# Six slots from chunk 3 to chunk 2, three from chunk 4 to chunk 3, chunk 3 turned by matmuls, and a new order of all queues

## Chip, core and metric

The kernel runs on one core of a Trainium2 chip. The metric is the device time of one execution in microseconds (us). An execution takes a little longer than the span of its trace, which runs from the first to the last instruction.

## The reference, cut to what matters

The inputs are x, r_gate and i_gate (4 x 5056 x 256), a_param (256), and a layer of 8 experts with 1024 hidden features, all float32.

```python
a    = exp(8 * sigmoid(r_gate) * log(sigmoid(a_param)))      # per token and feature
g    = sqrt(max(1 - a*a, 1e-6)) * sigmoid(i_gate) * x
h[t] = a[t] * h[t-1] + g[t]                                  # along the 5056 tokens of a sequence
e_idx = argmax(h @ w_gate)                                   # one of 8 experts for each token
out   = softmax(h @ w_gate)[e_idx] * sigmoid(h @ w_output_gate)[e_idx]
        * (relu(h @ w1[e_idx]) @ w2[e_idx])                  # 20224 tokens, 256 -> 1024 -> 256
```

## The kernel before, in words

**Chunks.** The 20224 tokens are 158 tiles of 128, worked in chunks: chunks 0 and 1 have 4 tiles each, every further one 8. For a chunk, SP loads r, i and x (L752). ACT makes the gates (L758, L761), the decay (L768), its square (L772) and the root (L777; ACT needs another function table for it). DVE multiplies (L764, L780) and runs the scan (L812). PE and DVE then find a power-of-two scale (for the first four chunks L836, L842, L845, L852 to L859).

**Turning rows.** The scan has features on the partitions, while the slots gather tokens as rows of `rows_all`, in two float16 parts (high and low). There are two ways. Chunks below `BY_PE` are turned by matmuls with a stationary scan tile and a moving identity (`project`, L932), which brings the routing logits with it. ACT takes the high part out of PSUM (L948) and DVE the low part (L951, L952). The other chunks are split in place by ACT (L972) and DVE (L977, L979), SP turns the halves by a transposing DMA, called a flip below (L988), and PE makes the logits by other matmuls (L996), gathered by DVE (L1004). Either way 12 tile rows of `rows_all` take turns.

**Routing.** DVE and ACT choose the expert and its probability (L1035 to L1080), PE counts ranks (`pk`, L1053, L1055), DVE makes positions (L1086 to L1093), and POOL scatters the 8 tiles' rows to `xs` in HBM, by expert (L545).

**Slots.** A slot is up to 128 rows (256 in the later sets) of one expert. SP fetches it with a transposing DMA (L1234) and its scales (L1235). A table `SETS` has entries (chunk, first expert, end expert, rows): one slot of so many rows for each of the experts, which may start once the chunk of that number is scattered. Chunks are counted from 0, here and below, so `(3, 0, 8, 128)` is a slot for each expert behind the fourth chunk. Rows that are left go to 16 end slots and 3 half end slots of 64 rows (`ENDS`, `HALVES`). The slots of set 0 (slots 0 to 7) are plain: they use the expert's weights in float32 as they are loaded (L1276, L1292, L1327, L1367). The others use two float16 parts: 48 matmuls L1306, relu on ACT (L1331), low part on DVE (L1334), 24 matmuls L1381 for each 128 rows, result on ACT (L1402), store by POOL (L1405).

**Weights.** Unit 2e is w1 of expert e, unit 2e+1 its w2. Each is loaded (L601, by ACT's queue for the first seven, by SP for the others), squared up on PE, ACT and DVE (`pg`: L627, L633, L636, L641) to find its scale, and split on ACT and DVE (L669, L679). Units 14 and 15 are loaded in four pieces (`fw14_0` to `fw15_1`) into the ring of the plain slots' hidden tiles.

**Order.** Every queue is worked in the order in which it was filled. The works are collected first; `places` gives each a rank from a table, and `in_order` lists them by rank with a model of the engines' time.

Of the kernel before, what the change touches and what calls it, by code (L numbers as in the profile page):

```python
# [1534 lines left out]
```

## Time and profile before

| | |
|---|---|
| median of 3 runs | 1009.37 us (1009.24 to 1009.70) |
| profiled execution | 1010.89 us |
| its span, granted TensorE clock | 1009.0 us, 0.977 of full |
| PE busy | 940.9 us (93%) |
| DVE, ACT, POOL busy | 678.2, 624.1, 359.9 us |

The chain that ended last is made of PE to 59%, DVE 13%, ACT 11% and DMA 10%. PE's last matmul ends at 1000.35 us and its first slot starts at 69.25 us. Read the page's 40 slices from left to right: PE is filled from the fourth on, with one dip in the slice from 126 to 151 us, where PEclk falls to 8 tenths too. Clock 0.50 in a stretch is the lower of two levels, 1.2 and 2.4 GHz.

### The profile page before, as it was taken

What the parts mean: (1) busy time and instruction counts of PE and PEld (TensorE: products, weight loads), DVE (VectorE), ACT (ScalarE), POOL (GpSimd) and SP (SyncE); (2) the same over time, 40 slices, a digit from 0 to 9 for tenths busy, and PEclk for the clock granted to TensorE, in tenths of its full rate; (3) what the DMA queues carried; (4) which work ended last, traced back from release to release, by engine and by line L of the source; (5) the groups of instructions that cost most, each with busy time, mean ns of one, the idle gap of its engine ahead of it and who ended that gap; (6) DMA issues with size and microseconds to landing.
All of it is one profiled execution on the core that took longest, in us unless ns stands there. A gap on an engine that the chain in (4) does not pass through costs nothing.

```text
span 1009.0 us, 27629 instructions
## 1 busy us (share of the span) xinstructions
PE 940.9 (93%) x10796; PEld 860.5 (85%) x10796; DVE 678.2 (67%) x1719; ACT 624.1 (62%) x931; POOL 359.9 (36%) x341
## 2 busy tenths in 40 slices
PE   1389959999999999999999999999999999999996
PEld 1379859998999899999888888988888888899994
DVE  5789998888978898889878987878322222322231
ACT  8799987877777688877778777743322322322321
POOL 2115252544444444445344554444221211221111
PEclk9779988999999999999999999999999999999998
DMA  9999997989999999899988898656522122138771
GB/s 318 338 264 330 241 211 184 218 191 221 212 222 200 209 253 255 166 228 221 249 179 224 203 250 210 122 125 208 113 52 53 48 54 49 47 111 229 247 232 37
DMA packets 269237, 189.75 MB, mean 188 GB/s; under 512 B 211071, under 2 KB 222080, under 8 KB 269104
## 3 DMA queue, kind: packets, MB, share of 16 engines
q1 hardware_dynamic: 249488, 138.37, 59.5%
q0 software_dynamic: 15408, 42.22, 13.7%
q10 hardware_dynamic: 4208, 7.34, 2.0%
q8 instruction: 88, 1.44, 0.6%
q14 instruction: 45, 0.37, 0.1%
HBM read 79.09 MB, written 44.82 MB: 123 GB/s over the span
## 4 chain that ended last, share of the span: by engine, by line
PE 59%; DVE 13%; ACT 11%; DMA 10%; issue 4%; POOL 1%; SPq 1%; ACTq 0%; POOLq 0%; DVEq 0%
PE po L1381 27%; PE ph L1306 27%; DMA out_dram<-ot,osc 3%; DVE it L812 3%; DVE h L1334 3%; DMA it<-in_i_gate_dram 3%; PE po L1367 2%; DVE it L780 2%; ACT it L772 2%; ACT it L777 1%; ACT L777 1%; PE ph L1292 1%; DVE peak L864 1%; DVE xt L764 1%; DMA fw<-in_moe_w_dram 1%
## 5 line engine op out<-in xcount | busy, mean ns | idle before, releaser
L1381 PE MATMUL po<-w2r,h 128*128 128x256 f16 (+2 forms) x3720 | 494.5, 273 | 2.8 <-ACT ot L1402 1.3
L1306 PE MATMUL ph<-xt,w1r 128*128 128x128 f16 (+1 forms) x4608 | 427.1, 241 | 3.9 <-DMA xt<-xs 3.0
L1381 PEld LDWEIGHTS <-h 128*128 128x128 f16 (+1 forms) x3720 | 347.5, 98 | 41.9 <-issue 3.5
L1306 PEld LDWEIGHTS <-w1r 128*128 128x128 f16 x4608 | 349.2, 98 | 30.5 <-DMA xt<-xs 3.4
L1334 DVE SCALAR_TENSOR_TENSOR h<-ph,h 128x512 f16<-128x512 f32 (+1 forms) x310 | 208.3, 680 | 225.6 <-ACT h L1331 222.8
L1331 ACT ACTIVATE h<-ph 128x512 f16<-128x512 f32 (+1 forms) x310 | 180.6, 588 | 253.0 <-PE ph L1306 156.6
L1405 POOL DMA_INDIRECT out_dram<-ot,osc x163 | 174.9, 1073 | 424.7 <-ACT ot L1402 367.0
L545 POOL DMA_INDIRECT xs<-rows_all,posi x158 | 180.0, 1139 | 207.5 <-ACT h L1331 93.9
L1402 ACT ACTIVATE ot<-po,osc 128x256 f32<-128x256 f32 (+1 forms) x163 | 73.2, 469 | 62.2 <-PE po L1381 41.1
L812 DVE TENSOR_TENSOR_SCAN it<-rt,last,it 128x512 f32<-128x512 f32 (+4 forms) x78 | 96.1, 1241 | 0.5
L780 DVE SCALAR_TENSOR_TENSOR it<-it,xt 128x1024 f32<-128x1024 f32 (+1 forms) x40 | 48.3, 1208 | 28.9 <-ACT it L777 28.9
L768 ACT ACTIVATE rt<-rt,lam 128x512 f32<-128x512 f32 (+1 forms) x80 | 62.5, 803 | 2.4 <-issue 1.7
L1306 PE MATMUL ph<-xt,ws 128*128 128x128 f16 (+1 forms) x912 | 63.8, 215 | 0.0
L764 DVE SCALAR_TENSOR_TENSOR xt<-it,xt 128x1024 f32<-128x1024 f32 (+1 forms) x40 | 48.2, 1205 | 18.1 <-ACT it L761 18.1
L1306 PEld LDWEIGHTS <-ws 128*128 128x128 f16 x912 | 55.8, 98 | 4.1 <-issue 2.0
L761 ACT ACTIVATE it<-it 128x1024 f32<-128x1024 f32 (+1 forms) x40 | 41.5, 1040 | 16.1 <-DMA it<-in_i_gate_dram 16.1
L979 DVE SCALAR_TENSOR_TENSOR rt<-it,scale,rt 128x512 f16<-128x512 f32 (+1 forms) x76 | 48.9, 685 | 1.9 <-ACT rt L972 1.8
L772 ACT ACTIVATE it<-rt 128x1024 f32<-128x1024 f32 (+1 forms) x40 | 41.6, 1044 | 10.0 <-DVE xt L764 9.2
L758 ACT ACTIVATE rt<-rt 128x1024 f32<-128x1024 f32 (+1 forms) x40 | 41.7, 1043 | 9.3 <-DMA rt<-in_r_gate_dram 9.0
L777 ACT ACTIVATE it<-it,quarter 128x1024 f32<-128x1024 f32 (+1 forms) x40 | 44.8, 1134 | 0.3
L972 ACT ACTIVATE rt<-it,scale 128x1024 f16<-128x1024 f32 (+1 forms) x38 | 42.0, 1131 | 4.2 <-DVE scale L886 4.1
L864 DVE TENSOR_REDUCE peak<-it 128x1 f32<-128x1024 f32 (+1 forms) x34 | 40.0, 1193 | 0.0
(186 smaller groups left out, 694.1 us busy)
## 6 DMA issues: line engine op xcount, KB each, us to landing
rt<-in_r_gate_dram SPq DMA_DIRECT2D x39, 512.0 KB
it<-in_i_gate_dram SPq DMA_DIRECT2D x39, 512.0 KB
xt<-in_x_dram SPq DMA_DIRECT2D x39, 512.0 KB
ws<-w1r SPq DMA_DIRECT2D x38, 512.0 KB
w1r<-in_moe_w_dram ACTq DMA_DIRECT2D x4, 1024.0 KB
w2r<-in_moe_w_dram SPq DMA_DIRECT2D x4, 1024.0 KB
w2r<-in_moe_w_dram ACTq DMA_DIRECT2D x3, 1024.0 KB
w1r<-in_moe_w_dram SPq DMA_DIRECT2D x3, 1024.0 KB
```

Source lines behind the costliest of these rows:

```text
L545: op = nc.gpsimd.indirect_dma_start(out=xs[:, :], out_offset=bass.IndirectOffsetOnAxis(ap=pos, axis=0), in_=rows.bitcast(F32), in_offset=None,
L768: nc.scalar.activation(r[:, h], r[:, h], AF.Exp, scale=lam[:, h:h + 1], bias=lam[:, h:h + 1])
L772: nc.scalar.activation(t("it"), t("rt"), AF.Square)
L777: nc.scalar.activation(t("it"), t("it"), AF.Sqrt, scale=-0.25, bias=quarter)
L780: nc.vector.scalar_tensor_tensor(t("it"), t("it"), 0.5e-3, t("xt"), op0=ALU.max, op1=ALU.mult)
L812: nc.vector.tensor_tensor_scan(H[:, h, lo:hi], A[:, h, lo:hi], H[:, h, lo:hi], first, op0=ALU.mult, op1=ALU.add)
L1306: nc.tensor.matmul(ph[:, i, 0:w], lhsT=ws[:, f // 2 % 2, a, c, f % 2 * P:(f % 2 + 1) * P], rhs=xt[:, b * ND + c, 0:w], start=n == 0, stop= ...
L1331: newest["relu"] = nc.scalar.activation(part(0, f0), tiles["ph", s, f0][:, :, 0:w], AF.Relu).ins
L1334: nc.vector.scalar_tensor_tensor(part(1, f0), tiles["ph", s, f0][:, :, 0:w], 0.0, part(0, f0), op0=ALU.max, op1=ALU.subtract)
L1381: nc.tensor.matmul(po[0:pw, j], lhsT=hh[:, a, f % 4, j * P:j * P + pw], rhs=second(b), start=f + j + a + b == 0, stop=f == NF - 1 and a == ...
L1402: nc.scalar.activation(ot[0:pw], tiles["po", s][0:pw, j], AF.Copy, scale=tiles["osc", s][0:pw, j, 0:1])
L1405: op = nc.gpsimd.indirect_dma_start(out=out[:, :], out_offset=bass.IndirectOffsetOnAxis(ap=tiles["osc", s][0:pw, j, 1:2].bitcast(I32), axi ...
```

## The change

- `SETS`: (2, 0, 6, 128) gives experts 0 to 5 their second slot after chunk 2, where all eight had it after chunk 3; experts 6 and 7 keep theirs, and experts 3 to 5 get their third slot after chunk 3 too, where all eight had it after chunk 4; experts 0 to 2 and 6, 7 keep it there. All 104 such slots stay. Slots 8 to 13 are the six, 14 and 15 the two, 16 to 18 the three.
- `BY_PE` is a tuple: chunk 3 is turned by matmuls too.
- `ENDS` 16 to 19 and `HALVES` 3 to 0: the three half end slots have 128 rows.
- `PLAIN` names the same set. Line numbers fall by 5 from L752 on.
- `laid_out` reads the order of emission itself from a table; `in_order` is left for the loop after it only.

```diff
-SETS = [(1, 0, 8, 128), (3, 0, 8, 128), (4, 0, 8, 128), (5, 0, 8, 128), (6, 0, 8, 128), (8, 0, 8, 128), (9, 0, 8, 128), (10, 0, 8, 128),
+SETS = [(1, 0, 8, 128), (2, 0, 6, 128), (3, 6, 8, 128), (3, 3, 6, 128), (4, 0, 3, 128), (4, 6, 8, 128), (5, 0, 8, 128), (6, 0, 8, 128), (8, 0, 8, 128), (9, 0, 8, 128), (10, 0, 8, 128),
         (12, 0, 8, 256), (14, 0, 8, 256), (16, 0, 8, 256), (18, 0, 8, 256), (20, 0, 8, 256)]
-PLAIN = (0,)
+PLAIN = {0: 0}
-BY_PE = 2
+BY_PE = (0, 1, 3)
-ENDS = 16
-HALVES = 3
+ENDS = 19
+HALVES = 0
...
-        for b in range(0, nt, 4) if c < BY_PE else ():
+        for b in range(0, nt, 4) if c in BY_PE else ():
...
-    first = [w for w in works if not w.late]
-    for w, v in zip(first, places(len(first))):
-        w.rank = v
-
     engines = {PE, mybir.EngineType.Activation, mybir.EngineType.DVE}
     with tc.manual_schedule(engines=engines):
-        for w in in_order([w for w in works if not w.late], {"DVE": 1.7, "ACT": 0.8}):
-            w.emit()
+        for k in laid_out(len([w for w in works if not w.late])):
+            works[k].emit()
```

**ACT's queue at chunk 1.** Before; `rt_2_4`, `it_2_4` belong to chunk 2, `lg_1_0` and `prow_1_1` to `prow_1_3` to chunk 1, whose high parts are the four L948:

```order
L768 ACTIVATE rt_2_4_159<-rt_2_4_159,lam_94 128x512
L761 ACTIVATE it_2_4_273<-it_2_4_273 128x1024 [waits DMAHW4_49]
L601 DMA w1r_135<-in_moe_w1_dram 128x2x1024 [waits DMAHW2_49]
L948 ACTIVATE rows_all_134<-lg_1_0_339,scale_1_376 128x256 [waits DVE_49,PE_49]
L948 ACTIVATE rows_all_134<-prow_1_1_363,scale_1_376 128x256 [waits PE_49]
L948 ACTIVATE rows_all_134<-prow_1_2_280,scale_1_376 128x256
L948 ACTIVATE rows_all_134<-prow_1_3_319,scale_1_376 128x256
L772 ACTIVATE it_2_4_273<-rt_2_4_159 128x1024 [waits DVE_49]
L772 ACTIVATE it_2_0_154<-rt_2_0_156 128x1024
L1039 ACTIVATE ex_1_403<-df_1_401 128x32 [waits DVE_49]
L777 ACT_TABLE_LOAD
L777 ACTIVATE it_2_0_154<-it_2_0_154,quarter_92 128x1024 [waits Activation_49]
```

After; L943 is the high part, L756 the gate i, L596 a weight load:

```order
L763 ACTIVATE rt_2_4_193<-rt_2_4_193,lam_94 128x512
L756 ACTIVATE it_2_0_164<-it_2_0_164 128x1024
L943 ACTIVATE rows_all_131<-lg_1_0_342,scale_1_376 128x256 [waits DVE_49,PE_49]
L943 ACTIVATE rows_all_131<-prow_1_1_373,scale_1_376 128x256 [waits PE_49]
L943 ACTIVATE rows_all_131<-prow_1_2_380,scale_1_376 128x256 [waits PE_49]
L943 ACTIVATE rows_all_131<-prow_1_3_386,scale_1_376 128x256 [waits PE_49]
L596 DMA w2r_133<-in_moe_w2_dram 128x8x256 [waits DMAHW3_49]
L756 ACTIVATE it_2_4_283<-it_2_4_283 128x1024 [waits DMAHW2_49]
L628 ACTIVATE dg_2_423,sq_2_424<-pg_2_398 128x128 [waits PE_49,Activation_49]
L767 ACTIVATE it_2_0_164<-rt_2_0_161 128x1024 [waits DVE_49]
L1034 ACTIVATE ex_1_434<-df_1_429 128x32 [waits DVE_49]
L763 ACTIVATE rt_2_4_193<-rt_2_4_193,lam_94 128x512
```

The four high parts stood behind the gate of `it_2_4`, which waits for its load, and behind a weight load. Now both stand behind them.

**PE's queue behind slot 7.** Before; `ph_7` is slot 7, `lg_4` are logits of chunk 4:

```order
L1292 MATMUL ph_7_4_1520<-xt16_7_1305,fw14_1_1456 128x128
L1292 MATMUL ph_7_4_1520<-xt16_7_1305,fw14_0_1438 128x128
L1292 MATMUL ph_7_4_1520<-xt16_7_1305,fw14_1_1456 128x128
L996 LDWEIGHTS rt_4_0_828
L996 MATMUL lg_4_0_1451<-g16_101,rt_4_0_828 128x48 [waits DVE_49]
L996 LDWEIGHTS rt_4_0_828
L996 MATMUL lg_4_0_1451<-g16_101,rt_4_0_828 128x48
L996 LDWEIGHTS rt_4_0_828 [waits DVE_49]
L996 MATMUL lg_4_0_1451<-g16_101,rt_4_0_828 128x32
```

After; `ph_8` is layer 1 of slot 8 (L1301), `lg_4_0<-dp_4` finds chunk 4's scale:

```order
L1287 MATMUL ph_7_4_1490<-xt16_7_1263,fw14_0_1404 128x128
L1287 MATMUL ph_7_4_1490<-xt16_7_1263,fw14_1_1415 128x128
L872 LDWEIGHTS ones_b_97
L872 MATMUL lg_4_0_1512<-dp_4_1500,ones_b_97 128x128 [waits DVE_49]
L1301 LDWEIGHTS w1r_132 [waits DMAHW4_49]
L1301 MATMUL ph_8_0_1514<-xt16_8_1425,w1r_132 128x128 [waits PE_49]
L1301 LDWEIGHTS w1r_132
L1301 MATMUL ph_8_0_1514<-xt16_8_1425,w1r_132 128x128
L1301 LDWEIGHTS w1r_132
```

Logits that wait for DVE stood behind slot 7. Now slot 8, of chunk 2's set, stands there, 36 matmuls of it in a row, and the logits come later.

**SP's queue between the fetches of slots 5 and 7.** Before; L988 are the flips of chunk 3:

```order
L1234 DMA_TRANSPOSE xt16_5_1074<-xs_84 128x4x128 [waits DMAHW0_49,DVE_49,PE_49]
L1235 ISA
L1235 DMA mt_5_1075<-xs_84 128x2 [waits DMAHW1_49]
L752 DMA it_4_4_1137<-in_i_gate_dram 128x2x512 [waits DMAHW2_49,DVE_49,Activation_49]
L988 DMA_TRANSPOSE rows_all_134<-rt_3_0_243 128x19x128 [waits DMAHW3_49,DVE_49,Activation_49]
L1223 TENSOR_LOAD firsti_0_447
L1234 ISA
L1234 DMA_TRANSPOSE xt16_6_1230<-xs_84 128x4x128 [waits DMAHW4_49,PE_49]
L1235 ISA
L1235 DMA mt_6_1231<-xs_84 128x2 [waits DMAHW5_49]
L988 DMA_TRANSPOSE rows_all_134<-rt_3_4_283 128x19x128 [waits DMASW5_49,DMASW4_49,DMAHW6_49,DMASW3_49,DMASW2_49]
L1223 TENSOR_LOAD firsti_0_447
```

After, from slot 5's fetch on:

```order
L1229 DMA_TRANSPOSE xt16_5_976<-xs_84 128x4x128 [waits DMAHW3_49,DVE_49,PE_49]
L1230 ISA
L1230 DMA mt_5_977<-xs_84 128x2 [waits DMAHW4_49]
L747 DMA xt_4_0_1026<-in_x_dram 128x2x512 [waits DMAHW5_49]
L747 DMA it_4_4_1044<-in_i_gate_dram 128x2x512 [waits DMAHW6_49,PE_49]
L596 DMA w1r_132<-in_moe_w1_dram 128x2x1024 [waits DMAHW7_49]
L747 DMA xt_4_4_1070<-in_x_dram 128x2x512 [waits DMAHW0_49]
L596 DMA w2r_133<-in_moe_w2_dram 128x8x256 [waits DMAHW1_49]
L1218 TENSOR_LOAD firsti_0_475
L1229 ISA
L1229 DMA_TRANSPOSE xt16_6_1129<-xs_84 128x4x128 [waits DMAHW2_49,DVE_49,PE_49]
```

The two flips are gone; loads of chunk 4 and of weights stand in their place.

## Rows read from the trace of the kernel before

**Rows 1.** By stretch: us; busy PE, PEld, DVE, ACT, POOL; PEclk, DMA share, GB/s.
```profile
60.00:130.00 70.00, 66.58 (x621) 62.26 (x620) 65.19 (x151) 66.84 (x97) 22.69 (x18) 0.97 1.05 266
130.00:160.00 30.00, 19.21 (x172) 17.00 (x171) 25.61 (x43) 25.18 (x30) 11.34 (x6) 0.77 0.91 202
...
300.00:700.00 400.00, 398.11 (x4710) 364.17 (x4708) 338.50 (x866) 288.55 (x421) 186.12 (x170) 1.00 0.89 205
```

**Rows 2.** Timeline of ACT (start, duration, instruction, idle before and releaser).
```profile
36.88 1.06 ACT L761 ACTIVATE it<-it 128x1024 f32<-128x1024 f32 x1 [1.68 <-DMA it<-in_i_gate_dram]
36.89 3.71 ACTq L601 DMA_DIRECT2D w1r<-in_moe_w_dram  x1
40.70 0.47 ACT L948 ACTIVATE rows_all<-lg,scale 128x256 f16<-128x256 f32 x1 [2.76 <-issue]
...
46.75 1.28 ACT L1067 ACT_TABLE_LOAD   x1
```

**Rows 3.** Timeline of PE at the first slot.
```profile
66.80 1.69 PE L627 MATMUL pg<-w1r 128*128 128x128 bf16 x16
...
69.25 3.82 PE L1292 MATMUL ph<-xt,w1r 128*128 128x128 f32 x32
```

**Rows 4.** Timeline of PE, its five waits between 130 and 160 us.
```profile
134.78 0.64 PE L627 MATMUL pg<-fw 128*128 128x128 bf16 x8 [1.80 <-DMA fw<-in_moe_w_dram]
...
143.66 0.21 PE L996 MATMUL lg<-g,rt 128*128 128x32 bf16 x1 [3.95 <-DVE rt L979]
144.32 0.61 PE L996 MATMUL lg<-g,rt 128*128 128x32 bf16 x13 [0.45 <-DVE rt L979]
146.73 1.46 PE L1306 MATMUL ph<-xt,w1r 128*128 128x128 f16 x12 [1.81 <-DMA xt<-xs]
...
151.84 1.03 PE L627 MATMUL pg<-fw 128*128 128x128 bf16 x8 [2.79 <-DMA fw<-in_moe_w_dram]
```

**Rows 5.** By stretch, in slices of 5 us.
```profile
140.00:145.00 5.00, 0.82 (x14) 0.61 (x14) 5.00 (x10) 4.66 (x6) 1.33 (x1) 0.82 0.67 157
145.00:150.00 5.00, 2.32 (x20) 2.05 (x20) 4.86 (x11) 3.88 (x5) 1.23 (x1) 0.50 0.98 166
150.00:155.00 5.00, 3.16 (x15) 2.76 (x16) 1.71 (x4) 1.93 (x4) 0.00 (x0) 0.50 0.82 115
```

**Rows 6.** Timeline of PE, turning by matmuls (L932) and logits behind flips (L996).
```profile
31.39 0.71 PE L932 MATMUL lg<-iw,it 128*128 128x144 f32 x4
31.93 0.65 PE L932 MATMUL prow<-iw,it 128*128 128x144 f32 x4
...
98.94 0.62 PE L996 MATMUL lg<-g,rt 128*128 128x48 bf16 x16
```

**Rows 7.** Timeline of SP's queue, a flip of chunk 3 and a load.
```profile
102.26 6.98 SPq L988 DMA_TRANSPOSE rows_all<-rt  x1
...
118.19 0.39 SPq L752 DMA_DIRECT2D rt<-in_r_gate_dram  x1
```

**Rows 8.** Timeline of PE, full end slots, then the last half slot.
```profile
953.45 0.49 PE L1381 MATMUL po<-w2r,h 128*128 x3
953.78 1.50 PE L1306 MATMUL ph<-xt,ws 128*128 128x128 f16 x24
955.12 0.49 PE L1381 MATMUL po<-w2r,h 128*128 x3
...
991.64 0.35 PE L1306 MATMUL ph<-xt,ws 128*128 128x64 f16 x6
...
995.90 4.45 PE L1381 MATMUL po<-w2r,h 128*64 x36
```

**Rows 9.** Timeline of POOL and SP: last scatter of chunk 8, first fetch of its slots.
```profile
319.34 0.97 POOL L545 DMA_INDIRECT xs<-rows_all,posi  x1 [0.31 <-DVE osc L1349]
...
329.53 1.57 SPq L1234 DMA_TRANSPOSE xt<-xs  x1
```

**Rows 10.** Timeline of POOL, first scatter of chunk 2.
```profile
86.95 0.97 POOL L545 DMA_INDIRECT xs<-rows_all,posi  x1 [2.92 <-DVE osc L1349]
```

More of the change, by code (lines that the diff above doesn't have):

```diff
@@ L336, in rglru_moe @@
     NF = F // P
-    assert GRAMS >= BY_PE and D == 2 * P and E == 8 and F == 8 * P and N % P == 0 and N + (FILLS + 1) * P <= REGION and max(w for *_, w in SETS) <= FILLS * P
+    assert GRAMS > max(BY_PE) and D == 2 * P and E == 8 and F == 8 * P and N % P == 0 and N + (FILLS + 1) * P <= REGION and max(w for *_, w in SETS) <= FILLS * P
     chunks = []
@@ L744, in load @@
                 bufs = rings[tags[k]].n
-                wide_ = c >= BY_PE and tags[k] == PLANES
+                wide_ = c not in BY_PE and tags[k] == PLANES
                 t = pool.tile(
@@ L854, in level @@
             )
-            if c >= BY_PE:
+            if c not in BY_PE:
                 inv = small.tile([P, 1], I32, name=f"inv_{c}", tag="inv")
@@ L901, in chunk @@
             en = work("PE", 0.25, energy, [mo], EARLY + c / 100, uses=[pu0], slack=SLACK[c > 4])
-            le = work("DVE", 0.3 + 0.15 * (c >= BY_PE), level, [en], late_rank, uses=[pu0])
+            le = work("DVE", 0.3 + 0.15 * (c not in BY_PE), level, [en], late_rank, uses=[pu0])
         else:
@@ L1213, in slot @@
         ready, vuse = planned[s] if expert is None else (counted[c], again_used[group])
-        plain = set_of[s] in PLAIN
+        plain = expert is not None and expert >= PLAIN.get(set_of[s], E)
         scaled = None if expert is None or plain else undone[expert]
@@ L1326, in relu @@
                         tiles["hh", s, 0] = wk.tile([P, NF, P], F32, name=f"h_{s}", tag="hh")
-                    newest["relu"] = nc.scalar.activation(tiles["hh", s, 0][:, f0:f0 + g], tiles["ph", s, f0], AF.Relu).ins
+                    newest["relu"] = nc.scalar.activation(tiles["hh", s, 0][:, f0:f0 + g, 0:w], tiles["ph", s, f0][:, :, 0:w], AF.Relu).ins
                     return
@@ L1346, in scales @@
             again = tiles["again", s][0:pw] if expert is None else tiles["again", group][0:pw, place, 0:q]
-            by = tiles["scale", s][0:pw] if expert is None else 1.0 if plain else tab[:, 2, expert:expert + 1]
+            by = tiles["scale", s][0:pw] if expert is None else 1.0 if plain else tab[0:pw, 2, expert:expert + 1]
             nc.vector.tensor_scalar(osc[0:pw, 0:q, 0:1], tiles["mt", s][0:pw, 0:q, 0:1], by, None, op0=ALU.mult)
@@ L1367, in multiply2 @@
                     nc.tensor.matmul(
-                        po[:, 0], lhsT=tiles["hh", s, 0][:, f], rhs=raw_of(2 * expert + 1, f * D, D), start=f == 0, stop=f == NF - 1,
+                        po[0:pw, 0], lhsT=tiles["hh", s, 0][:, f, 0:w], rhs=raw_of(2 * expert + 1, f * D, D), start=f == 0, stop=f == NF - 1,
                     )
```

143 lines of the change are left out of this document (69 added, 74 removed).

## The prediction

> **What bounds the kernel now.** I read the busy time by stretch first [rows 1]. From 300 to 700 us PE works 398.11 of 400 us at full clock: there every microsecond of PE work counts, and no wait is left to win. From 60 to 130 us it works 66.58 of 70. The exception is 130 to 160 us, with 19.21 of 30 and a clock of 0.77. So time can come from three places: before the first slot, in this hole, or from the amount of PE's work.
>
> The timeline of PE in the hole [rows 4] shows five waits, 1.80 + 3.95 + 0.45 + 1.81 + 2.79 = 10.80 us, all of the idle time there. Two are for pieces of the last expert's weights (`fw`, 4.59 us), two for the split of chunk 4 on DVE (4.40 us), one for the first rows of the slots behind chunk 3 (1.81 us). The clock is the second loss [rows 5]: behind the long wait it falls to 0.82 and then to 0.50, the lower level of 1.2 GHz. What work there was ran slower: 0.82 x 0.18 + (2.32 + 3.16) x 0.50 = 2.9 us. The hole costs 13.7 us.
>
> Before the first slot I read the timelines of ACT and PE. The slot's layer 1 starts at 69.25 [rows 3], behind the routing of chunk 1. That routing waits at 36.88 on ACT, where the gate of chunk 2 waits 1.68 us for its load, and the high parts of chunk 1 wait another 2.76 us behind a weight load that holds ACT's queue for 3.71 us [rows 2]. Later it waits again, for a table load of 1.28 us at 46.75.
>
> **The change part by part.** The sums are made against the profiled execution, 1010.89 us with a span of 1009.0. It is 1.5 us above the median of the runs, so I take 1.5 off at the end.
>
> *Start.* In the new ACT order the four high parts of chunk 1 stand ahead of that gate and that weight load. The waits ahead of them were 1.68 + 2.76 = 4.44 us [rows 2]. The probability sum `zs` also stands ahead of the table switch, which saves its reload, 1.28 us. Together 5.7 us. Against it, three weight loads in a row now stand on ACT ahead of the high parts of chunk 0, each behind the landing of an earlier transfer; the one such issue that the rows show took 3.71 us. Ends: 5.7 us won, 3.7 us lost. Slot 0 also follows, on PE, the squares of unit 6 at 66.80 [rows 3]; if their weights land no earlier, only 69.25 - 66.80 = 2.5 us can be won without them. I take 4.0 won: nearer the ACT rows, because the waits there are seen, and because slot 0 no longer needs what stood ahead of chunk 1. From 60 to 130 us PE is 95% busy [rows 1], so a shift at its beginning is carried to the hole.
>
> *The hole.* Six slots behind chunk 2 can now fill it. Chunk 2's scatter begins at 86.95 [rows 10], some 50 us ahead of the hole, so these rows are not waited for. In the PE order slot 8 stands right behind slot 7, and the logits of chunk 4 come later. The two waits for DVE (4.40) and the one for rows (1.81) go: 6.2 us. What is late next there is `fw`: slot 7 still needs its weights, and the second piece of w2 needs the buffer of `fw14_0`, free only after slot 7's layer 1. I leave both waits in, 4.59 us; if they go too, the sum is that much lower. With two short waits and float16 slots between them I expect the clock to hold: 2.9 us. The hole gives 6.2 + 2.9 = 9.1 us, between 6.2 (the clock falls anyway) and 13.7.
>
> *Chunk 3 by matmuls.* Four records of L932 make one tile, and two batches start 31.93 - 31.39 = 0.54 us apart [rows 6]: 8 tiles, 4.3 us. The logits that fall away are 32 of L996, and 16 took 0.62 us: 1.2 us. PE gets 3.1 us more, all on the path, since the stage around it is 95% filled. On ACT eight high parts of about 0.4 to 0.47 us [rows 2] stand against two wide ones, one to two microseconds more; DVE's low parts take about what the split and the gathering took. Neither is on the path while slots wait in stock.
>
> *Flips.* One held SP's queue for 6.98 us, a load for 0.39 us [rows 7]. I give their removal nothing: the waits for `fw` are waits for buffers, and the other waits of the hole are counted already. If the free queue brought the weights earlier, it would win the 4.59 us above; if loads merely go out into a full DMA, nothing. The Trainium skill (Advanced Engine Details and Errata, X-Bar Transpose (TRN2)) says that transposing DMAs are as fast as regular ones, which would make the removal worth no more than dropping a load of the same size. The rows show the queue held far longer, though not how long the bytes took. By the rule the sum stays as it is; by the rows it could be 4.6 us lower.
>
> *Ends.* The last half slot: from 991.64 to 995.90 run 48 of L1306 and 15 of L1381, and 36 of L1381 take 4.45 us, 0.124 each [rows 8]. So the 48 take 4.26 - 15 x 0.124 = 2.4, and a half slot 2.4 + 24 x 0.124 = 5.4 us. A full one: 24 of L1306 take 955.12 - 953.78 = 1.34, three of L1381 953.78 - 953.45 = 0.33, so 48 and 24 take 2.7 + 2.6 = 5.3 us. Halving the rows saved nothing; three full ones for three half ones cost 0, within 0.3 us either way.
>
> *Order of the rest.* From 300 us on PE has under 0.5% idle [rows 1]. A new order can lose there, hardly gain; I take 0.
>
> Sum: 1010.9 - 4.0 - 9.1 + 3.1 = 1000.9, less 1.5: **999.4**. Its own range is 993 (the `fw` waits go too, full start gain) to 1004 (clock falls, half the start gain).
>
> **The rivals.**
> - *Supply gives the lead back.* PE arrives some 10 us earlier at every later chunk, while DVE, ACT and DMA must keep up. The tightest place I found is chunk 8: its last scatter starts at 319.34 and takes 0.97, the first fetch of its slots is at 329.53 [rows 9]: 9.2 us of slack. If DVE and ACT don't come earlier at all, the lead ends at 9.2 us; if they come later by the 4 us of the longer queues and matmul turning, at 5.2, so 1009.4 - 5.2 = 1004.2. For it: DMA is 0.89 busy there. Against: DVE has 61 of 400 us free [rows 1], and most scatters wait for pacing, not for rows.
> - *No gain.* The start stays, because PE waits for weights of unit 6 instead, and in the hole the `fw` waits grow by what the others lose, 6.2 us. Then only the clock, 2.9, stands against 3.1: 1009.6.
> - *Slower.* The high parts of chunk 3 need the `rows_all` places of chunk 2's first tiles, so they wait on ACT for scatters that begin at 86.95 [rows 10], and behind them wait weight splits and a relu of the plain slots. It decides if PE brings chunk 3's tiles before that. Waiting from some 79 to 87 costs 8 us at a place where PE has no stock; with 3.1 for the matmuls, the start unmoved, and the hole's 6.2 won back: 1009.4 + 8 + 3.1 - 6.2 = 1014.3.
> - *More work on the fullest engine.* PE is the fullest engine, and 3.1 us are added to it; if PE's idle time only moves elsewhere, the result is 1009.4 + 3.1 = 1012.5. The Trainium skill (Perfetto Trace Analysis, Identifying the Most-Contended Engine) says to optimize the engine of highest occupancy first, and by that work should leave PE. The hole in rows 1 speaks against its use here: PE is not full in the stage that gets the work.
>
> **How the numbers follow.** Forecast 0.60 (993 to 1004), supply 0.13 (about 1004), no gain 0.10 (1008 to 1011), slower by ACT's wait 0.10 (1014), slower by added work 0.07 (1012). The first two are faster, and a third of the third: 0.76. A measurement of this kernel can tell 0.2%, 2 us, from no change; same 0.07, slower 0.17. The range that leaves out two in ten runs from 990 to 1011: it cuts both slower cases and some of the low end.
>
> **What would show it.** Slot 0 near 65 us, and the high parts of chunk 1 on ACT without the 4.4 us ahead of them. In the hole no wait for DVE's split or for rows, slot 8 right behind slot 7, clock 1.00 throughout, and at most two waits for `fw`. Eight L932 tiles of 0.54 us. After 300 us idle time of PE of 2 us, as before. I am wrong if PE waits for rows of chunk 8 or 9, if ACT waits for a scatter at chunk 3's high parts while PE idles, or if the first slot starts after 69 us.

## The result

The changed kernel took 999.55 us (median of 4, 999.23 to 1002.18), the kernel before beside it 1009.54. The ratio is 0.9903, with a 95% interval of 0.9882 to 0.9924. The profiled execution took 999.23 us with a span of 997.5 us, 11.5 us less than the 1009.0 us of before; the medians are 10.0 us apart, since the profiled execution of before was 1.5 us above its median.

The same view by stretch as in [rows 1] (columns: us; busy PE, PEld, DVE, ACT, POOL; granted clock, DMA share, GB/s), of the changed kernel:

```profile
60.00:130.00 70.00, 67.75 (x583) 62.39 (x583) 65.40 (x141) 64.67 (x95) 26.28 (x17) 1.00 0.92 256
130.00:160.00 30.00, 26.91 (x342) 24.04 (x342) 29.06 (x74) 27.17 (x37) 13.70 (x11) 1.00 0.95 211
160.00:300.00 140.00, 135.54 (x1952) 126.84 (x1950) 128.86 (x325) 111.96 (x157) 67.12 (x61) 1.00 0.99 231
300.00:700.00 400.00, 396.95 (x4638) 363.42 (x4636) 330.21 (x842) 291.25 (x422) 183.97 (x168) 1.00 0.86 198
```

From 130 to 160 us PE works 26.91 us where it worked 19.21, and the clock is 1.00 where it was 0.77. The last two rows show the price. From 160 to 300 us the row of before was this one:

```profile
160.00:300.00 140.00, 137.04 (x1971) 128.94 (x1969) 120.16 (x306) 106.20 (x152) 64.45 (x57) 1.00 0.91 204
```

There DVE is now busy 128.86 us for 120.16, and PE has 4.46 us without work where it had 2.96. From 300 to 700 us PE has 3.05 us without work where it had 1.89.

PE's time without work, stretch by stretch of the same view, adds up to the result:

| stretch, us | before | changed | difference |
|---|---|---|---|
| 0 to 130 | 43.7 | 36.4 | -7.3 |
| 130 to 160 | 10.8 | 3.1 | -7.7 |
| 160 to 700 | 4.9 | 7.5 | +2.7 |
| 700 to the end | 8.8 | 8.4 | -0.4 |
| PE busy | 940.9 | 942.1 | +1.2 |
| span | 1009.0 | 997.5 | -11.5 |

PE's timeline behind slot 7, which answers to [rows 4]:

```profile
126.95 0.63 PE L622 MATMUL pg<-fw 128*128 128x128 bf16 x8 [0.21 <-DMA fw<-in_moe_w_dram]
...
129.71 3.73 PE L1287 MATMUL ph<-xt,fw 128*128 128x128 f32 x32
133.28 0.22 PE L872 MATMUL lg<-dp,ones_b 128*128 128x128 bf16 x1
133.34 0.50 PE L1301 MATMUL ph<-xt,w1r 128*128 128x128 f16 x6
135.36 1.83 PE L1301 MATMUL ph<-xt,w1r 128*128 128x128 f16 x30 [1.52 <-ACT h L1322]
137.03 1.27 PE L622 MATMUL pg<-fw 128*128 128x128 bf16 x16
...
140.85 0.49 PE L991 MATMUL lg<-g,rt 128*128 128x32 bf16 x13 [0.31 <-DVE rt L974]
```

Slot 7's layer 1 (L1287) is followed by slot 8's (L1301). The wait for the last weights is 0.21 us where 1.80 and 2.79 stood, the wait for DVE's split 0.31 where 3.95 and 0.45 stood, and nothing waits for rows. One new wait is there: 1.52 us at 135.36 for ACT, where a relu frees PSUM.

The start:

```profile
58.68 3.60 PE L1287 MATMUL ph<-xt,w1r 128*128 128x128 f32 x24 [0.28 <-DVE xt L1271]
```

Slot 0 begins at 58.68 us, 10.6 us before 69.25 [rows 3].

### The profile page after: what moved, and what is told of

Read it like the earlier page. It is cut to its first block, busy times and chain, and to the rows that moved or that the text cites. A ratio compares the mean times of both kernels' runs of the same rounds, so it can differ in the third digit from the quotient of the medians.

```text
span 997.5 us, 27694 instructions
## 1 busy us (share of the span) xinstructions
PE 942.1 (94%) x10796; PEld 863.5 (87%) x10796; DVE 684.5 (69%) x1739; ACT 630.4 (63%) x941; POOL 360.2 (36%) x340
## 4 chain that ended last, share of the span: by engine, by line
PE 65%; DVE 4%; DMA 3%; ACT 3%; issue 2%; POOL 0%; SPq 0%; POOLq 0%; ACTq 0%; DVEq 0%
PE ph L1301 32%; PE po L1376 32%; DMA it<-in_i_gate_dram 2%; DVE it L807 1%; DMA out_dram<-ot,osc 1%; PE lg L991 1%; DVE h L1329 1%; ACT h L1326 1%; ACT rt L967 1%; DVE it L775 0%; ACT it L772 0%; ACT L772 0%; DVE peak L859 0%; DMA xs<-rows_all,posi 0%; ACT it L767 0%
## 5 line engine op out<-in xcount | busy, mean ns | idle before, releaser
L1376 PE MATMUL po<-w2r,h 128*128 128x256 f16 (+1 forms) x3720 | 491.3, 272 | 2.3 <-DVE h L1329 1.7
L1301 PE MATMUL ph<-xt,w1r 128*128 128x128 f16 (+1 forms) x4608 | 426.2, 241 | 5.2 <-DVE h L1329 2.3
L1376 PEld LDWEIGHTS <-h 128*128 128x128 f16 x3720 | 348.2, 98 | 42.6 <-DVE h L1329 3.9
L1301 PEld LDWEIGHTS <-w1r 128*128 128x128 f16 x4608 | 350.7, 98 | 32.2 <-issue 4.7
L1329 DVE SCALAR_TENSOR_TENSOR h<-ph,h 128x512 f16<-128x512 f32 x310 | 210.0, 686 | 225.6 <-ACT h L1326 225.0
L1326 ACT ACTIVATE h<-ph 128x512 f16<-128x512 f32 x310 | 181.8, 593 | 263.7 <-PE ph L1301 191.8
L1400 POOL DMA_INDIRECT out_dram<-ot,osc x163 | 183.5, 1126 | 386.5 <-ACT ot L1397 328.0
L540 POOL DMA_INDIRECT xs<-rows_all,posi x158 | 171.7, 1087 | 235.2 <-ACT h L1326 99.0
L1397 ACT ACTIVATE ot<-po,osc 128x256 f32<-128x256 f32 x163 | 73.1, 469 | 50.6 <-PE po L1376 37.4
L1301 PE MATMUL ph<-xt,ws 128*128 128x128 f16 x912 | 68.9, 219 | 0.0
L1301 PEld LDWEIGHTS <-ws 128*128 128x128 f16 x912 | 60.1, 98 | 2.6
L759 DVE SCALAR_TENSOR_TENSOR xt<-it,xt 128x1024 f32<-128x1024 f32 (+1 forms) x40 | 48.3, 1208 | 14.9 <-ACT it L756 13.9
L767 ACT ACTIVATE it<-rt 128x1024 f32<-128x1024 f32 (+1 forms) x40 | 41.8, 1045 | 11.1 <-DVE xt L759 10.8
L756 ACT ACTIVATE it<-it 128x1024 f32<-128x1024 f32 (+1 forms) x40 | 41.7, 1043 | 11.0 <-DMA it<-in_i_gate_dram 9.1
L967 ACT ACTIVATE rt<-it,scale 128x1024 f16<-128x1024 f32 (+1 forms) x36 | 39.5, 1130 | 3.4 <-DVE scale L881 3.3
```

The costliest lines, as they stand in the source:

```text
L540: op = nc.gpsimd.indirect_dma_start(out=xs[:, :], out_offset=bass.IndirectOffsetOnAxis(ap=pos, axis=0), in_=rows.bitcast(F32), in_offset=None,
L759: nc.vector.scalar_tensor_tensor(t("xt"), t("it"), 1.0, t("xt"), op0=ALU.add, op1=ALU.mult)
L967: nc.scalar.activation(halves(key, 0, m // P), of_tiles(key, m), AF.Copy, scale=tiles["scale_of", c])
L1301: nc.tensor.matmul(ph[:, i, 0:w], lhsT=ws[:, f // 2 % 2, a, c, f % 2 * P:(f % 2 + 1) * P], rhs=xt[:, b * ND + c, 0:w], start=n == 0, stop= ...
L1326: newest["relu"] = nc.scalar.activation(part(0, f0), tiles["ph", s, f0][:, :, 0:w], AF.Relu).ins
L1329: nc.vector.scalar_tensor_tensor(part(1, f0), tiles["ph", s, f0][:, :, 0:w], 0.0, part(0, f0), op0=ALU.max, op1=ALU.subtract)
```

## The experiments

Twelve runs were made in three groups of four. A group shares a chip and its runs of the kernel before, and the chips differ: that kernel took 1018.6 us in the first group, 1019.96 in the second and 1008.55 in the third. All ratios are to the kernel before of the same group. Two groups hold the changed kernel itself as a control; the first doesn't, and its ratios can only be held against a control of another chip. Where an order is changed, the diff names the works in the order of emission.

**Controls: the changed kernel again.** No edit.

> The changed kernel itself, as a control beside the three below, since chips differ: the four runs before this one stood beside runs of the kernel before that took 1018.6 us, not 1009.4. Theory A: a chip shifts both kernels alike, so the ratio is 0.990 again. Rival: the gain rests on transfers and waits that take other times on another chip; then the ratio lies nearer to 1 (0.995 to 1.003).

> The changed kernel once more, as control of this group, on a chip that may be another one. Theory S, the supply gives the lead back: the start and the hole are won on every chip (PE idle ahead of 160 us lower by 12 to 14 us than in the kernel before), and how much of it is left at the end depends on how fast chunks are made behind 160 us; so the ratio lies anywhere from 0.990 to 1.002, with PE's idle time between 160 and 700 us higher in proportion: 7.5 us at 0.990, about 20 us at 1.00. Rival: the start or the hole themselves differ between chips.

Measured: on the second group's chip 1019.27 us, ratio 1.0015 (0.9991 to 1.0039), so no gain at all; on the third's 999.11 us, ratio 0.9906 (0.9884 to 0.9928), the result again. The kernel before is slower on the second chip too, by 11.4 us (1019.96 for 1008.55). Here are the two controls by stretch, the one without the gain first:

```profile
0.00:60.00 60.00, 25.96 (x210) 23.18 (x211) 44.54 (x146) 48.73 (x68) 11.04 (x26) 0.83 0.93 322
...
130.00:160.00 30.00, 26.59 (x335) 23.79 (x334) 29.02 (x68) 26.12 (x36) 13.50 (x10) 1.00 0.88 209
160.00:300.00 140.00, 129.80 (x1821) 119.85 (x1820) 122.80 (x320) 105.70 (x147) 64.95 (x58) 1.00 0.94 218
300.00:500.00 200.00, 193.76 (x2626) 178.83 (x2624) 163.98 (x400) 153.85 (x215) 87.63 (x80) 1.00 0.96 210
500.00:700.00 200.00, 196.41 (x1971) 175.36 (x1969) 159.40 (x398) 139.44 (x208) 92.86 (x83) 1.00 0.77 183
```

```profile
0.00:60.00 60.00, 25.61 (x213) 22.95 (x214) 44.18 (x146) 48.40 (x68) 11.04 (x26) 0.89 0.92 322
...
130.00:160.00 30.00, 26.81 (x342) 24.05 (x342) 29.06 (x74) 27.19 (x37) 13.69 (x11) 1.00 0.94 211
160.00:300.00 140.00, 135.95 (x1961) 127.43 (x1959) 129.34 (x328) 112.66 (x158) 67.69 (x62) 1.00 0.98 231
300.00:500.00 200.00, 197.85 (x2623) 184.31 (x2622) 171.90 (x433) 157.76 (x221) 88.40 (x81) 1.00 0.96 215
500.00:700.00 200.00, 200.00 (x2019) 179.78 (x2017) 159.43 (x416) 133.45 (x201) 95.98 (x87) 1.00 0.77 184
```

Ahead of 160 us PE is without work for 41.0 us in the first and 40.4 in the second (3.5 and 2.8 of it from 60 to 130 us), against 54.4 in the kernel before: start and hole are won on either chip. Behind it the chips part: from 160 to 700 us 10.2 + 6.2 + 3.6 = 20.0 us in the first and 4.1 + 2.2 = 6.2 us in the second. When theory S was written, the second chip's 20 us and the 7.5 us of the result were already known, so the one new number is the 6.2 us at a ratio of 0.9906, and it fits. The kernel with full ends below, which stands for the kernel before on the second chip, has 53.2 us ahead of 160 us and 11.5 from 160 to 700: of the 12 us won there, 8.5 are given back behind 160 us, and 3 go into PE's busy time. The gain differs by some 10 us between this chip and that of the result: 5.8 of them lie from 160 to 700 us, 2.8 ahead of 160 us and 2.0 in PE's busy time.

What PE waited for from 160 to 700 us (waits by line: us in total, times, longest; the second chip's control, then the changed kernel of the result):

```profile
PE ph L1301 <- issue: 6.3, 12, 1.2
PE ph L1301 <- DVE h L1329: 5.8, 11, 1.0
PE po L1376 <- issue: 3.6, 9, 1.2
```

```profile
PE ph L1301 <- DVE h L1329: 2.3, 5, 1.0
```

On the second chip 10.2 us are waits for nothing that the profile shows ("issue"); the full-ends kernel has 6.0 us of them there, the changed kernel of the result none. 5.8 us are waits for the low parts that DVE makes, and none is for rows. So it isn't shown that transfers are slower on that chip, and why the lead is given back there is open.

**The start alone.**

```diff
 kernel before, order of emission
-its own, throughout
+that of the changed kernel up to slot 0's first matmul, then its own
```

> The kernel before with one part of the change: the order of emission of the changed kernel up to the first matmul of slot 0, and from there its own old order, written as a table. Slots, flips and ends as before. Theory A: slot 0 starts about 10 us sooner and PE has 7 us less idle time ahead of 130 us; the hole stays or grows by the part of the lead that its loads don't follow. Ratio 0.993 to 0.998. Rival: the hole takes all of it, because the last weights and chunk 4's split come no sooner: ratio 0.999 to 1.002.

Measured: ratio 1.0007 (0.9980 to 1.0034). Slot 0 has to be compared on the chip of this group. By PE's timeline it begins at 66.26 us in the full-ends kernel, at 63.84 in this run and at 58.50 in the control, in this order:

```profile
66.26 3.82 PE L1292 MATMUL ph<-xt,w1r 128*128 128x128 f32 x32
```

```profile
62.97 1.01 PE L627 MATMUL pg<-sq,ones 128*128 128x1 f32 x4 [0.65 <-ACT dg L624]
63.84 6.73 PE L1283 MATMUL ph<-xt,w1r 128*128 128x128 f32 x32
```

```profile
58.50 3.48 PE L1287 MATMUL ph<-xt,w1r 128*128 128x128 f32 x24 [0.28 <-DVE xt L1271]
```

So the edit won 2.4 us of the 7.8 that the whole change wins here. Slot 0's join on DVE began at 57.98 us, as early as in the changed kernel (58.21), but in the old order 32 logits of chunk 2 and squares stand ahead of slot 0 on PE, and they wait 1.63 + 0.49 + 0.45 us for DVE and 0.65 for ACT. The other 5.3 us are thus won by slot 0's place in PE's order. Behind these waits slot 0's layer 1 runs at a granted clock of 0.50 and takes 6.73 us, where the full-ends kernel has 1.00 and takes 3.82: what follows it begins at 70.41 us, there at 69.91. The lead is gone before the hole, and the hole is as in the full-ends kernel (first line below; this run behind it):

```profile
141.20 0.19 PE L996 MATMUL lg<-g,rt 128*128 128x32 bf16 x1 [3.95 <-DVE rt L979]
```

```profile
142.37 0.21 PE L987 MATMUL lg<-g,rt 128*128 128x32 bf16 x1 [3.95 <-DVE rt L970]
...
150.68 1.03 PE L618 MATMUL pg<-fw 128*128 128x128 bf16 x8 [2.74 <-DMA fw<-in_moe_w_dram]
```

The ratio lies in the rival's range, but the run doesn't test the rival: theory A's condition, a start about 10 us sooner, wasn't met, and no lead reached the hole that the hole could have taken. Whether an earlier start alone would be worth something stays open.

**ACT's order at chunk 1.**

```diff
 changed kernel, ACT's order
-L943 x4 (chunk 1), L596 (w2 of expert 2), L756 (it_2_4)
+L596 (w2 of expert 2), L756 (it_2_4), L943 x4 (chunk 1)
```

> The changed kernel with one thing moved on ACT: the weight load and the gate of chunk 2's second half stand ahead of chunk 1's four high parts again, as before. Theory A, these two waits made the start: the high parts start some 4 us later (about 38 us in place of 33.85), slot 0 4 us later, the end 3 to 5 us later: 1003 to 1004 us. Rival: the place of slot 0's join on DVE and of its first layer on PE made most of it, and what is late here is won back before 130 us: under 1 us slower.

Measured: ratio 1.0035 (1.0013 to 1.0057), without a control on that chip. The trace decides more than the time. ACT's timeline of this kernel, and of the changed one:

```profile
34.72 1.06 ACT L756 ACTIVATE it<-it 128x1024 f32<-128x1024 f32 x1 [1.41 <-DMA it<-in_i_gate_dram]
34.73 0.38 ACTq L596 DMA_DIRECT2D w2r<-in_moe_w_dram  x1
35.69 0.46 ACT L943 ACTIVATE rows_all<-lg,scale 128x256 f16<-128x256 f32 x1
...
41.33 0.21 ACT L1062 ACTIVATE zs<-zs 128x4 f32<-128x4 f32 x1
```

```profile
33.85 0.47 ACT L943 ACTIVATE rows_all<-lg,scale 128x256 f16<-128x256 f32 x1 [0.17 <-DVE scale L854]
...
37.56 1.06 ACT L756 ACTIVATE it<-it 128x1024 f32<-128x1024 f32 x1 [1.87 <-DMA xt<-in_x_dram]
...
41.63 0.19 ACT L1062 ACTIVATE zs<-zs 128x4 f32<-128x4 f32 x1
```

The high parts come 1.8 us later (35.69 for 33.85; ahead of 60 us the changed kernel's order runs alike in three groups of runs, with slot 0 at 58.68, 58.50 and 58.67), but the gate comes 2.8 us sooner (34.72 for 37.56), and `zs`, which closes chunk 1's routing, runs at 41.33 for 41.63; slot 0 starts at 58.45. So the order of these two did not make the start: DVE multiplies by that gate (L759) in the middle of chunk 1's routing, so what one gains the other loses. Theory A falls for this order. The edit didn't bring the waits themselves back: the weight load that now stands ahead is another one and held ACT's queue for 0.38 us, not 3.71, so of the 4.44 us only the 1.41 of the gate's wait stand there again. What those 4.44 us were worth is therefore not shown. Against the kernel before, `zs` runs 6.4 us sooner (41.63 for 48.05) and slot 0's join on DVE 9.1 us sooner (58.21 for 67.33); that slot 0 could follow the join at once is, by the run of the start alone, its place in PE's order.

**The nine slots undone.**

```diff
-SETS = [(1, 0, 8, 128), (2, 0, 6, 128), (3, 6, 8, 128), (3, 3, 6, 128), (4, 0, 3, 128), (4, 6, 8, 128),
+SETS = [(1, 0, 8, 128), (3, 0, 6, 128), (3, 6, 8, 128), (4, 3, 6, 128), (4, 0, 3, 128), (4, 6, 8, 128),
```

> The changed kernel with the nine slots back at their old chunks (six wait for chunk 3 again, three for chunk 4); everything else, and the order as far as the new waits allow, as in the changed kernel. Theory A, the slots fill the hole: PE has nothing behind slot 7 but chunk 4's logits, which wait for DVE, and then chunk 3's rows. The hole comes back with 5 to 8 us of idle time between 120 and 160 us and some 2 to 3 us of lower clock: 1006 to 1010 us. Rival, the order did it (weights and splits come sooner, so the old slots are in time too): under 2 us slower, 1000 to 1001.5.

Measured: 1040.79 us, ratio 1.0207 (1.0180 to 1.0235), some 20 us over a control of another chip (1.0015).

```profile
145.20 1.03 PE L622 MATMUL pg<-fw 128*128 128x128 bf16 x8 [5.56 <-DMA fw<-in_moe_w_dram]
...
159.93 6.19 PE L1301 MATMUL ph<-xt,w1r 128*128 128x128 f16 x72 [7.08 <-DMA xt<-xs]
```

Above is PE's timeline. It waits 5.56 us for the last weights and 7.08 us for rows, and is without work for 13.4 of the 30 us behind 130. That is the hole again, and deeper: theory A in kind, twice its size. The order was chosen for the new slots and has nothing else to offer there. No flip stands ahead of the last weights on SP's queue here, whose four pieces go out in a row from 124.92 to 139.00 us, and still PE waits for them.

**The nine slots alone.**

```diff
 kernel before, each work with its old rank, ordered by the old model
-SETS = [(1, 0, 8, 128), (3, 0, 8, 128), (4, 0, 8, 128),
+SETS = [(1, 0, 8, 128), (2, 0, 6, 128), (3, 6, 8, 128), (3, 3, 6, 128), (4, 0, 3, 128), (4, 6, 8, 128),
```

> The kernel before with one part of the change: the nine slots one chunk earlier, each work with the rank that it had, ordered by the old model. Start, flips and half ends as before. Theory A: slot 8 no longer waits for rows (1.8 us), and part of the waits for DVE's split and of the lower clock go: ratio 0.993 to 0.997. Rival: with the logits and the weights in their old places the same waits end the hole: ratio 0.998 to 1.003.

Measured: 1086.7 us, ratio 1.0671 (1.0628 to 1.0713). Both theories missed. The hole from 130 to 160 us shrank (PE 21.43 us busy for 19.27 in that group's full-ends kernel), but from 160 to 300 us PE worked 119.23 of 140 us and from 300 to 500 us 167.24 of 200: by the waits from 160 to 700 us, 16.2 us were for the low parts of the splits on DVE, 13.3 for relus on ACT and 12.6 for results on ACT. Ranks that were tuned for the old slots leave the new ones without their splits and relus. The slots alone are worth less than nothing; they need the order.

**Logits ahead of slot 8.**

```diff
 changed kernel, PE's order
-ph_7, ph_8 (36 of 48), pg_15, po_7 with logits of chunk 4
+ph_7, pg_15, po_7 with logits of chunk 4, ph_8
```

> The changed kernel with one thing moved on PE: the logits of chunk 4 and the second layer of slot 7 stand ahead of slot 8's first layer again, as before. Theory A: PE waits for chunk 4's split on DVE, 3 to 5 us, with slot 8's rows at hand, and the clock may fall: 1003 to 1006 us. Rival: what follows is limited by DVE and ACT anyway, so the wait is won back within the next chunk: under 1 us slower.

Measured: ratio 1.0042 (1.0014 to 1.0070), 0.0027 over a control of another chip, so the time can't tell. PE's timeline shows a wait, not the one I named:

```profile
134.66 0.64 PE L622 MATMUL pg<-fw 128*128 128x128 bf16 x8 [0.40 <-DMA fw<-in_moe_w_dram]
138.41 0.63 PE L622 MATMUL pg<-fw 128*128 128x128 bf16 x8 [3.11 <-DMA fw<-in_moe_w_dram]
```

PE waits 3.11 us for the last weights, which slot 8's 36 matmuls had covered, and not for DVE. The load itself is hardly later than in the changed kernel (134.3 for 133.5 us).

**The last weights late.**

```diff
 changed kernel, SP's order
-fw15_0, fw15_1, xt_5_4, fetches of slots 9 and 10, it_5_4, flip of chunk 4
+fw15_0, xt_5_4, fetches of slots 9 and 10, it_5_4, flip of chunk 4, fw15_1
```

> The changed kernel with one load moved on SP: the second half of the last expert's w2 stands behind the first flip of chunk 4 and the fetches ahead of it, as before. Theory F, the place on SP's queue made the waits for these weights: PE waits for them 2 to 6 us at the squares of unit 15, with the clock falling if the wait is long, and the time is 2 to 6 us over the control. Rival: the buffer, free only behind slot 7, sets when they come; the wait stays under 1 us.

Measured: 1011.28 us, ratio 1.0026 (1.0011 to 1.0040), 12.2 us over the control of its own group. The squares of unit 15 and what depends on them stand a little later on PE too, since they follow the load. PE's timeline and SP's:

```profile
137.06 0.26 PE L991 MATMUL lg<-g,rt 128*128 128x48 bf16 x2 [2.10 <-ACT rt L967]
...
149.73 1.04 PE L622 MATMUL pg<-fw 128*128 128x128 bf16 x8 [7.46 <-DMA fw<-in_moe_w_dram]
```

```profile
140.01 5.53 SPq L983 DMA_TRANSPOSE rows_all<-rt  x1
145.59 0.57 SPq L596 DMA_DIRECT2D fw<-in_moe_w_dram  x1
```

The load goes out at 145.59, behind a flip that holds SP's queue for 5.53 us; PE waits 7.46 us, the clock from 130 to 160 us is 0.72 and PE works 18.20 of these 30 us. Theory F is shown for this place, and its price is twice what I gave it. One load's place on SP's queue carries as much as the whole change, with all the new slots in stock.

Where the load leaves on time, the rival is right too. In the kernel before it left behind a flip and a fetch of rows, at 146.01 us, though slot 7's layer 1 had freed its buffer at 139.26; in the changed kernel it left at 133.5, the moment that slot 7's layer 1 ended (129.71 + 3.73 = 133.44). SP's timelines, before and changed (there the second of the two):

```profile
135.59 5.44 SPq L988 DMA_TRANSPOSE rows_all<-rt  x1
...
146.01 0.37 SPq L601 DMA_DIRECT2D fw<-in_moe_w_dram  x1
```

```profile
129.95 3.92 SPq L596 DMA_DIRECT2D fw<-in_moe_w_dram  x2
```

So before, the queue held the load 6.8 us longer than the buffer did. In the changed kernel the buffer holds it, and slot 8's matmuls cover the rest: 0.21 us of waiting is left, and 3.11 without them.

**Flips back.**

```diff
-BY_PE = (0, 1, 3)
+BY_PE = (0, 1)
 SP's order: in the first run the flips of chunk 3 stand ahead of the loads of units 12 and 13,
 in the second behind them
```

> The changed kernel with chunk 3 turned by flips again (its splits, flips, logits and gathering put where the matmuls, high and low parts stood). Theory A, the prediction's: PE does 3.1 us less and the flips cost nothing on the path, so 996 to 997 us. Rival B: the flips hold SP's queue for some 10 us where the last weights and the next loads are queued, and the chunk's scatter waits for them; PE waits 3 to 6 us more than it saves: 1002 to 1005.

> The changed kernel with chunk 3 turned by flips again, as in the second run, but the two flips stand behind the two weight loads on SP that they held up there (those were issued at 102.4 us, and PE waited 3.8 us at 101 us for that expert's scale). Theory Q, the queue: the weights come in time, that wait is gone, and the kernel lies 3 us or more under the second run's ratio of 1.010, near the control. Rival M, the bytes: the flips' transfers delay the weights wherever they stand, and the ratio stays within 0.002 of the second run's.

Measured: ahead of the loads 1.0102 (1.0075 to 1.0130), no control on that chip; behind them 1000.44 us, ratio 0.9930 (0.9906 to 0.9953), 1.3 us over its control, which is within the intervals. The first ran on another chip than the second. In the first, PE's timeline shows it waiting for that expert's scale, and SP's timeline the load behind the flips:

```profile
101.08 4.63 PE L1362 MATMUL po<-w2r,h 128*128 128x256 f32 x10 [3.76 <-DVE wsq L636]
```

```profile
102.42 0.57 SPq L596 DMA_DIRECT2D w1r<-in_moe_w_dram  x1
```

In the second 0.49 us of that wait are left, though the two flips hold SP's queue for 17.53 us (SP's timeline):

```profile
87.06 0.73 SPq L596 DMA_DIRECT2D w1r<-in_moe_w_dram  x1
...
89.09 1.12 SPq L596 DMA_DIRECT2D w2r<-in_moe_w_dram  x1
91.68 17.53 SPq L983 DMA_TRANSPOSE rows_all<-rt  x2
```

By the ratios theory Q holds (1.0102 and 0.9930), with the reserve that they stand on two chips. By the trace its cause isn't shown: the wait ends at 101.08 us, before the load that the flips held up goes out at 102.42. The scale stood on DVE behind a gathering of logits that began at 100.09 us, after 3.09 us of waiting for something that the profile doesn't name. The matmuls cost PE 3.2 us more than the flips' logits (on the third chip L927 takes 5.2 us more, L991 2.0 less), and yet the kernel with flips isn't faster than the control but 1.3 us slower in the median: PE is without work for 5.2 us from 60 to 130 us, at a granted clock of 0.98, for 2.8 at 1.00 in the control. By the medians, taking the flips away is thus worth what the matmuls cost and a little more, some 4.5 us with an interval of about 3 us, and not nothing.

**Full ends alone.**

```diff
-ENDS = 16
-HALVES = 3
+ENDS = 19
+HALVES = 0
```

> The kernel before with 19 end slots of 128 rows in place of 16 and 3 half ones, nothing else. Theory A, by the pitch of the matmuls: a half slot takes PE 5.4 us and a full one 5.3, so within 0.5 us of the kernel before: ratio 0.9995 to 1.0005. Rival: three full ones cost 0.5 us more each in layer 1 and in the stores: ratio 1.001 to 1.002.

Measured: ratio 1.0002 (0.9980 to 1.0024). Theory A stands; the rival's 1.001 to 1.002 lies inside the interval too.

**Thin peaks.**

```diff
-                tiles["peak", c][:, b // 4:b // 4 + 1], tiles["it", key][:, :, 0:m], axis=AX.XY, op=ALU.max, apply_absolute_value=True
+                tiles["peak", c][:, b // 4:b // 4 + 1], tiles["it", key][:, :, 0:m // 4], axis=AX.XY, op=ALU.max, apply_absolute_value=True
```

> The changed kernel with a probe: the peak that sets a chunk's scale is taken over the first quarter of each block's tokens, so that DVE has some 0.9 us less for each of 34 reductions, 30 us in all (three quarters of the peak's input are left out). Theory S1, DVE is what gives the lead back: PE's idle time behind 160 us falls by 5 us or more and the time lies 4 to 10 us under the control. Rival S2, transfers or the issue of PE's instructions give it back: within 2 us of the control.

Measured: 995.88 us (994.54 to 996.85), ratio 0.9872 (0.9851 to 0.9894), 3.2 us under the control. DVE was busy 24 us less up to 985 us, but PE's time without work from 160 to 700 us fell from 6.2 to 5.0 us only; the rest of the profile's gain lies ahead of 160 us. The intervals of the two ratios overlap (0.9884 to 0.9928 for the control). The sign is for relief on DVE, but the probe can't part S1 from S2: on this chip only 6.2 us were there to be won, and the chip that gives 20 us away wasn't probed. As a version it would need a bound on what the left tokens may hold.

## Why the prediction was right, step by step

The time, 999.4 for 999.55, is closer than its terms. The main mechanism is the one that was forecast: slot 8 in the hole, no wait for DVE's split or for rows there, and the clock held.

- **The start, 4.0 us won.** It was 7.3 us of PE's time without work, beyond the 5.7 us end. The step that named ACT's two waits as the cause isn't borne out: with their order put back slot 0 starts where it did (58.45), though only 1.41 of their 4.44 us came back with it. What the runs show in its place is PE's order, 5.3 of 7.8 us on the second group's chip; the prediction had slot 0's place behind the squares of unit 6 as a limit only. The sentence that a shift is carried to the hole wasn't tested: the start alone lost its lead by 70 us.
- **The hole, 6.2 us of waits and 2.9 of clock.** 7.7 us and a clock of 1.00. The waits for DVE and for rows went as said. The clock's 2.9 us left out 155 to 160 us, where PE was busy 5.00 us at 0.81, another 0.95. The step that left the two waits for `fw` in failed: 4.59 us were 0.21. I took them for waits for buffers. Before, the place on SP's queue made the last one, 6.8 us beyond the buffer; in the changed kernel the buffer does set when the load leaves, and slot 8's matmuls cover it.
- **Matmuls for chunk 3, 3.1 us.** By the lines of the third group's control and of its kernel with flips it is 3.2 us. PE's busy time rose by 1.2 us, where 3.1 of work less 2.9 of clock would have made 0.2. The other 1.0 us lies elsewhere; one row that grew is layer 1 of the slots ahead of slot 7 (30.9 us for 27.2); slot 0 now begins where the granted clock is still 0.50 (55 to 60 us).
- **Flips, nothing.** Too low: worth 4 to 4.5 us by one pair of kernels, the lower end by their profiles. The row that showed SP held for 6.98 us [rows 7] was the one to go by. By the Trainium skill (Advanced Engine Details and Errata, X-Bar Transpose (TRN2)) a transposing DMA is as fast as a regular one; the traces don't say how long the bytes took, but the queue was held for 17.53 us by two of them, while the two loads of weights ahead of them held it for 0.73 and 1.12 us.
- **Ends, nothing.** 1.0002 agrees.
- **Order behind 300 us, nothing.** 1.2 us were lost from 300 to 700 us, and 1.5 from 160 to 300, for which no term stood. This is the rival of the supply in small, but not at its named place: chunk 8's last scatter now starts at 308.01 us, 11.3 sooner than in [rows 9]. A wait for rows at chunk 8's slots, which the prediction had named as a sign of being wrong, is there once, 1.23 us at the last of them, 53 us behind that scatter; the kernel before had one like it, 1.16 us at 240.47, which is gone:

```profile
361.18 0.51 PE L1301 MATMUL ph<-xt,w1r 128*128 128x128 f16 x6 [1.23 <-DMA xt<-xs]
```

- **Slower by ACT's wait for scatters.** It didn't come. Chunk 3's eight high parts stand at 84.39 to 94.30 us; the longest wait among them is for PE, and the one for a scatter is 0.18 us:

```profile
89.41 0.47 ACT L943 ACTIVATE rows_all<-prow,scale 128x256 f16<-128x256 f32 x1 [1.48 <-PE prow L927]
```

So two terms were too small on the winning side, by 3.3 and 1.5 us, and two on the losing side, by 2.3 (from 160 us to the end) and 1.0 (PE's busy time). They cancel to 1.5 us: between the profiled executions the time fell by 11.7 us, where the terms add up to 10.0. That the time came out within 0.2 us is luck on top of that: 1.5 us were taken off because the profiled execution of before lay above its median, and the profile of the changed kernel did not. On the second group's chip the same sum would have been 10 us wrong; there the lead was given back, as the supply rival says, but by waits whose cause is open and not by rows that came late.

## What to carry to other kernels

Work taken forward into a hole pays only together with an order that has its loads, splits and relus in place: here the slots alone cost 6.7%, and one load moved back on SP's queue cost 12.2 us. An earlier start has to be followed through every engine's order: with the old order on PE, slot 0 kept 2.4 of 7.8 us. When a stage waits for a transfer, compare the time at which its buffer came free with the time at which its load went out: 6.8 us apart the queue held it, nothing apart the buffer did. And when the lead is won, ask which stage must keep it: the same kernel was 0.94% faster on one chip and not at all on another, and more than half of the difference lay behind the part that was changed.

## What the runs showed of the hardware that was not expected

Chips differ by more than this change: the kernel before took 1008.6 to 1020 us in four groups of runs on three chips at least, and the changed one 999.1 to 1019.3. On one of them it gained 0.94%, on another nothing. Two transposing DMAs in a row held SP's queue for 17.53 us, against 6.98 for one in the kernel before.
